# The last batch's stores on GpSimd's queue, and two indirect transfers without an order between them, in an attention and mixture-of-experts kernel

## The chip, the cores and the metric

The kernel runs on one core of one Trainium2 chip. The metric is device microseconds for one execution of the whole program; lower is better. A profile of one execution stands beside the times. Its span runs from the first to the last recorded instruction, and the execution's own time is a little longer than its span.

## The reference

The kernel computes multi-query attention and, on its output, a mixture of experts with a two-step gate. In the reference, cut to what matters:

```python
scores = scale * q @ k.T                       # 8 batches, 16 heads, 384 tokens, head size 64; one k and v per batch
x = softmax(scores) @ v                        # as [3072 tokens, 1024]
g_idx = argmax(x @ w_group)                    # one of 4 groups, weight g_w = its softmax
e_idx = argmax(x @ w_expert[g_idx])            # one of 4 experts in it, weight e_w = its softmax
out[token] = g_w * e_w * (relu(x @ w1[g, e]) @ w2[g, e])
```

Inputs and outputs are float32. Every token goes to exactly one of 16 experts.

## The kernel before, in words

**Attention.** Work goes through 24 tiles of 128 tokens (8 batches, `ST` = 3 tiles each). A written-out loop (L792) runs scores, softmax, transposition and the product with `v` for half a head group at a time; gate steps and loads are hung into its slots with `at`.

**Experts.** For each batch the kernel counts which expert most of a sample of its tokens choose, and runs all 384 tokens of the batch through this one expert; tokens of another expert get the gate value 0 and so rows of zeros. `main_expert` (L535) is a generator: 8 groups of matmuls for the hidden layer (L483, evicted at L489), then for each token tile `j` two halves of 512 columns, each 8 matmuls (L497), evicted into a tile `y` of [128, 1024] float32 by ScalarE (L515) or VectorE (L517). It yields three times for each such group, and `advance(n)` takes `3 * n` steps, so `advance(1)` is one group of 8 matmuls on TensorE. When a tile is complete, `store` (L538) writes it in four transfers of 32 rows, one for each `n`, because token rows lie interleaved: `out_v = out.rearrange("(b j r n) d -> b j n r d", n=4, r=32)`. SP issues them; for the very last tile ScalarE's queue issues two of the four.

**The last batch** has a second expert as well. Up to 32 tokens that chose it are gathered (`few_gather`, L649), run through its weights with the 32 tokens as the stationary side (`few_rows`, L672, called twice in `few_expert`, L683), and their rows are written by an indirect transfer (L694) that takes one row number per partition: 32 tokens by four quarters of a row. It stands after the main expert's stores and overwrites the zero rows that these wrote. `few_places` (L620) computes on VectorE where each of these tokens goes and whether they fit (`fits32`); `few_parts` (L641) and the gate values run on GpSimd.

**Remaining pairs.** A loop at the end (L909) runs once for each pair of batch and expert that is still left; it reloads that batch's hidden input from `xb_scratch`, which `keep_xb` (L473) wrote. On these inputs no instruction of its body is recorded.

**Queues.** Weights are loaded by GpSimd's queue (L458; they are converted from float32 to bfloat16 on the way), which is DMA queue q0. SP's transfers are q1, those of ScalarE's queue q10. Instructions on an engine's queue run in order. The framework orders two transfers that may write the same bytes: the later waits on its issuing engine until the earlier has landed. `manual_schedule` keeps the program order as written.

**The end, in program order** (L888 to L906): `few_gather`, `advance(2)` (tile 0), the list of the remaining pairs, `advance(1000)` (tiles 1 and 2), `keep_xb`, `few_expert`, then the loop.

Of the kernel before, what the change touches and what calls it, by code (L numbers as in the profile page):

```python
# [11 lines left out]
I32 = mybir.dt.int32  # L12
P = 128
AX = mybir.AxisListType
ALU = mybir.AluOpType
ACTF = mybir.ActivationFunctionType
# [3 lines left out]
def kernel(  # L20
# [11 lines left out]
    nc = tc.nc  # L32
# [440 lines left out]
    def keep_xb(b):  # L473
        nc.sync.dma_start(out=xb_dram[b], in_=st["xb", b][:].rearrange("p c t -> p (c t)"))

    def expert(xb, w1, w2, result, psum, on_act=None):

        on_act = on_act or (lambda k: k % 2 == 0)
        h_t = pool.tile([P, FO, S], BF16, tag="hT", bufs=1)
        for fc in range(FO):  # L480
            hp = psum()
            for ko in range(KO):
                nc.tensor.matmul(  # L483
                    out=hp[:, 0:S], lhsT=w1[:, ko, ts(fc, P)], rhs=xb[:, ko, :], start=(ko == 0), stop=(ko == KO - 1)
                )
                if ko % (KO // 2) == KO // 2 - 1:
                    yield
            if on_act(fc):
                nc.scalar.activation(out=h_t[:, fc, :], in_=hp[:, 0:S], func=ACTF.Relu)  # L489
            else:  # L490
                nc.vector.tensor_scalar(out=h_t[:, fc, :], in0=hp[:, 0:S], scalar1=0.0, scalar2=None, op0=ALU.max)
            yield
        for j in range(ST):
            for nh in range(2):
                yp = psum()
                for fo in range(FO):
                    nc.tensor.matmul(  # L497
                        out=yp, lhsT=h_t[:, fo, ts(j, P)], rhs=w2[:, fo, ts(nh, 512)],
                        start=(fo == 0), stop=(fo == FO - 1),
                    )  # L500
                    if fo % (FO // 2) == FO // 2 - 1:
                        yield
                result(j, nh, yp, on_act(FO + 2 * j + nh))
                yield

    def scaled(gcol, store):

        ys = {}

        def result(j, nh, yp, by_act):  # L510
            if nh == 0:
                ys[j] = pool.tile([P, Dm], FP32, tag="y", name="y", bufs=3)
            y, g = ys[j], gcol()[:, j:j + 1]
            if by_act:
                nc.scalar.activation(out=y[:, ts(nh, 512)], in_=yp, func=ACTF.Copy, scale=g)  # L515
            else:
                nc.vector.tensor_scalar(out=y[:, ts(nh, 512)], in0=yp, scalar1=g, scalar2=None, op0=ALU.mult)  # L517
            if nh == 1:
                store(j, y)

        return result
# [13 lines left out]
    def main_expert(b, on_act):  # L535
        w1, w2 = st.pop(("w", b))

        def store(j, y):  # L538
            for n in range(QN):
                queue = nc.scalar if b == B - 1 and j == ST - 1 and n % 2 else nc.sync  # L540
                queue.dma_start(out=out_v[b, j, n], in_=y[32 * n:32 * (n + 1), :])

        yield from expert(st["xb", b], w1, w2, scaled(lambda: st["gsel", b][0], store), any_bank, on_act)

    def few_ready():

        c16 = ppool.tile([P, 4 * S], BF16, tag="pr", name="c16")
        c32 = ppool.tile([P, 2 * S], FP32, tag="pr", name="c32")
        st["few"] = fw = {}
        for name, t, widths in (  # L550
            ("16", c16, (("eye", P), ("tri", P), ("sel", ST * P), ("f", 4), ("cum", 4), ("parts", 5 * ST))),
            ("32", c32, (
                ("cols", P), ("tri", P), ("prod", ST * GE), ("ohs", GE), ("rows", ST), ("rest", ST), ("row", 1), ("pos", 4),
                ("f", ST), ("fits", 1), ("fits4", 1), ("gate", 1), ("low", 1), ("at", 1), ("base", 1),
            )),
        ):
            at_ = 0
            for part, w in widths:
                fw[part + name] = t[:, at_:at_ + w]
                at_ += w  # L560
        nc.gpsimd.iota(
            fw["cols32"], pattern=[[0, FQ], [1, FEW]], base=0, channel_multiplier=0,
            allow_small_or_imprecise_dtypes=True,
        )
        nc.gpsimd.memset(fw["tri32"], 1.0)
        nc.gpsimd.affine_select(
            out=fw["tri32"], in_=fw["tri32"], pattern=[[1, P]], compare_op=ALU.is_gt, fill=0.0, base=0,
            channel_multiplier=-1,
        )
        nc.gpsimd.tensor_copy(out=fw["tri16"], in_=fw["tri32"])  # L570
        nc.gpsimd.tensor_copy(out=fw["eye16"], in_=ident[:])
        nc.gpsimd.memset(c16[:, 2 * P + ST * P:2 * P + ST * P + 8], 0.0)

        rows, parts = fw["rows32"], fw["parts16"].rearrange("p (j t) -> p j t", t=5)
        nc.gpsimd.iota(
            rows, pattern=[[P, ST]], base=(B - 1) * S - NR, channel_multiplier=QN, allow_small_or_imprecise_dtypes=True
        )
        for n in range(QN):
            nc.gpsimd.memset(fw["low32"][32 * n:32 * (n + 1), :], float(n * (1 - 32 * QN)))
        for c in range(FQ):  # L580
            nc.gpsimd.memset(fw["base32"][ts(c, FEW), :], float(FQ * NR + c))
        nc.gpsimd.tensor_tensor(
            out=rows, in0=rows, in1=fw["low32"].to_broadcast([P, ST]), op=ALU.add
        )
        nc.gpsimd.tensor_copy(out=parts[:, :, 3], in_=rows)
        nc.gpsimd.tensor_tensor(out=parts[:, :, 4], in0=rows, in1=parts[:, :, 3], op=ALU.subtract)
        fw["xt"] = [ppool.tile([P, Dm], BF16, tag="pr", name="xtok") for _ in range(ST)]
        xg = ppool.tile([P, 2 * KO * FEW], BF16, tag="pr", name="xg")
        fw["xg"], fw["h16"] = xg[:, 0:KO * FEW], xg[:, KO * FEW:]
        rest = pool.tile([P, 512], FP32, tag="qt", name="rest", bufs=3)  # L590
        fw["h32"], fw["y32"] = rest[:, 0:KO * FEW], rest[:, KO * FEW:]
# [28 lines left out]
    def few_places():  # L620
        fw, ohs = st["few"], st["ohs", B - 1]
        bank = xbank()
        nc.tensor.matmul(out=bank[:, 0:4], lhsT=fw["tri16"], rhs=fw["f16"], start=True, stop=False)
        nc.tensor.matmul(out=bank[:, 0:4], lhsT=ones[:], rhs=fw["cum16"], start=False, stop=True)
        pos = fw["pos32"]
        nc.vector.tensor_copy(out=pos, in_=bank[:, 0:4])
        nc.vector.tensor_single_scalar(out=fw["fits32"], in_=pos[:, 3:4], scalar=float(FEW), op=ALU.is_le)
        nc.vector.tensor_scalar(
            out=fw["fits432"], in0=fw["fits32"], scalar1=float(FQ), scalar2=None, op0=ALU.mult
        )  # L630
        nc.vector.tensor_scalar(
            out=fw["ohs32"], in0=ohs[1], scalar1=fw["fits32"], scalar2=None, op0=ALU.mult
        )
        ohs[1] = fw["ohs32"]
        for j in range(ST):
            nc.vector.tensor_scalar(
                out=fw["sel16"][:, ts(j, P)], in0=fw["cols32"], scalar1=pos[:, j:j + 1], scalar2=fw["f32"][:, j:j + 1],
                op0=ALU.is_equal, op1=ALU.mult,
            )
# [40 lines left out]
                )  # L680
        return bank[:, 0:256]

    def few_expert():  # L683

        fw = st["few"]
        w1, w2 = st.pop("w_second")
        bank = few_rows(fw["xg"], w1)
        nc.vector.transpose(
            out=fw["h32"].rearrange("p (o t) -> p o t", t=FEW), in_=bank.rearrange("p (x o) -> p o x", o=FO)
        )  # L690
        nc.vector.tensor_scalar(out=fw["h16"], in0=fw["h32"], scalar1=0.0, scalar2=None, op0=ALU.max)
        bank = few_rows(fw["h16"], w2)
        nc.vector.tensor_scalar(out=fw["y32"], in0=bank, scalar1=fw["gate32"], scalar2=None, op0=ALU.mult)
        nc.gpsimd.indirect_dma_start(  # L694
            out=out_q, out_offset=bass.IndirectOffsetOnAxis(ap=fw["at32"].bitcast(I32), axis=0), in_=fw["y32"],
            in_offset=None, bounds_check=FQ * N - 1, oob_is_err=False,
        )
# [203 lines left out]
    nc.vector.tensor_copy(out=lsi[:, NP:NP + 1], in_=nsum[:])  # L901
    assert not later

    advance(1000)
    keep_xb(b)
    few_expert()  # L906

    n_rem = nc.values_load(lsi[0:1, NP:NP + 1], min_val=0, max_val=NP)
    with tc.For_i(0, n_rem, 1) as it:  # L909
        free.clear()  # L910
        e = nc.gpsimd.value_load(lse[0:1, ds(it, 1)], min_val=0, max_val=GE - 1)
        w1, w2 = load_w(e, 0), load_w(e, 1)
        bi = nc.sync.value_load(lsb[0:1, ds(it, 1)], min_val=0, max_val=B - 1)
        xr = pool.tile([P, KO, S], BF16, tag="xb", name="xr", bufs=2)
        nc.sync.dma_start(
# [44 lines left out]
```

## Time and profile before

| | us |
|---|---|
| three runs | 505.77, 508.03, 508.03 |
| median | 508.03 |
| the profiled execution | 507.47 |
| its span | 506.0 |

| engine | busy us | share of the span |
|---|---|---|
| TensorE, matmul | 479.9 | 95% |
| VectorE | 412.6 | 82% |
| ScalarE | 319.6 | 63% |
| GpSimd | 288.4 | 57% |

In the profile, PE is TensorE's matmuls and PEld its weight loads, DVE is VectorE, ACT ScalarE, POOL GpSimd, SP SyncE; a `q` behind the name is the engine's instruction queue (waits, DMA issues). A timeline line has the start, the length, the engine, the source line and the operation, the tile written and those read, shapes and a count; in brackets stands how long the engine sat idle before it, and what ended that. "DMA to landing" is the time from a transfer's start on the issuing engine to its completion signal. Tables of DMA queues give packets, MB and the time of the packets as a share of 16 DMA engines over the window.

### The profile page before, as it was taken

The numbers are of one execution on the slowest core, as the hardware profiler recorded it, in microseconds if no ns is written. First come the engines' busy times: TensorE is split into PE (matmuls) and PEld (weight loads), VectorE is DVE, ScalarE is ACT, GpSimd is POOL, SyncE is SP. The second block draws the span as 40 slices with busy tenths as digits, with TensorE's granted clock in tenths as the row PEclk, the third lists the DMA queues.
The fourth block names the chain that finished last, engine by engine and source line by source line (L and its number), as shares of the span: only waits on it lengthen the run. The fifth ranks groups of instructions, "written<-read, shape, count | busy, mean of one in ns | idle before, by whom it ended". The sixth has DMA issues, their size and how long they took to land.

```text
span 506.0 us, 20018 instructions
## 1 busy us (share of the span) xinstructions
PE 479.9 (95%) x8249; PEld 257.5 (51%) x8249; DVE 412.6 (82%) x738; ACT 319.6 (63%) x997; POOL 288.4 (57%) x528
## 2 busy tenths in 40 slices
PE   7687789999999999999999999999999999999992
PEld 3144355555455455555555455554555455555651
DVE  3899979998799888998799888898799888891441
ACT  4776756766765775766765875766766766662420
POOL 1656865585476654685476654684566653674210
PEclk9799999999999999999999999999999999999997
DMA  7522899389955999479965999279964995069995
GB/s 111 121 45 43 150 237 222 74 135 230 252 121 102 208 244 240 80 136 229 242 137 93 203 247 254 54 138 225 227 175 78 197 240 159 3 117 228 242 225 181
DMA packets 63660, 84.04 MB, mean 166 GB/s; under 512 B 20280, under 2 KB 39868, under 8 KB 63312
## 3 DMA queue, kind: packets, MB, share of 16 engines
q0 software_dynamic: 18288, 37.84, 41.2%
q1 hardware_dynamic: 44224, 44.35, 35.1%
q8 instruction: 66, 1.08, 0.9%
q10 hardware_dynamic: 1056, 0.56, 0.5%
q14 instruction: 26, 0.21, 0.1%
HBM read 101.52 MB, written 19.01 MB: 238 GB/s over the span
## 4 chain that ended last, share of the span: by engine, by line
PE 88%; DVE 4%; ACT 2%; DMA 2%; issue 1%; POOL 0%; SPq 0%; POOLq 0%; ACTq 0%; DVEq 0%
PE x L261 26%; PE s L210 26%; PE x L483 15%; PE x L497 13%; PE sb L497 3%; PE x L284 3%; ACT pr L224 2%; DVE nmx L221 2%; PE sb L483 2%; DMA out_dram<-y 2%; DVE ring L245 1%; PE x L104 1%; PE x L149 0%; PE x L187 0%; PE x L598 0%
## 5 line engine op out<-in xcount | busy, mean ns | idle before, releaser
L239 POOL TENSOR_SCALAR pr<-pr,rinv 128x384 f32<-128x384 f32 x384 | 217.3, 585 | 149.1 <-DVE rinv L235 135.9
L224 ACT ACTIVATE pr<-s,nmx 128x384 f32<-128x384 f32 x384 | 218.0, 579 | 132.2 <-DVE nmx L221 122.4
L221 DVE TENSOR_REDUCE nmx<-s 128x2 f32<-128x768 f32 x192 | 174.5, 949 | 47.2 <-PE s L210 46.3
L245 DVE STREAM_TRANSPOSE ring<-pr 128x768 f32<-128x768 f32 x192 | 175.4, 952 | 0.1
L210 PE MATMUL s<-kt,qt 64*64 64x384 f32 x1536 | 151.3, 504 | 12.0 <-ACT pr L224 9.9
L261 PE MATMUL x<-ring,v_sb 32*64 32x256 f32 x4608 | 137.9, 378 | 0.4 <-issue 0.3
L261 PEld LDWEIGHTS x<-ring,v_sb 32*64 32x64 f32 x4608 | 101.2, 131 | 43.7 <-issue 23.7
L210 PEld LDWEIGHTS s<-kt,qt 64*64 64x64 f32 x1536 | 48.8, 133 | 83.0 <-ACT pr L224 44.4
L224 ACT ACTIVATION_READ_ACCUMULATOR pr<-s,nmx 128x1 f32 x384 | 77.8, 203 | 0.0
L483 PE MATMUL x<-xb,w 128*128 128x384 bf16 x448 | 76.6, 326 | 0.0
L483 PEld LDWEIGHTS <-w 128*128 128x128 bf16 x512 | 47.7, 98 | 42.2 <-issue 12.6
L497 PE MATMUL x<-w,h_t 128*128 128x512 bf16 x288 | 65.3, 380 | 0.0
L497 PEld LDWEIGHTS <-h_t 128*128 128x128 bf16 x384 | 35.7, 98 | 51.9 <-issue 11.9
L458 POOL DMA_DIRECT2D w<-in_moe_w_dram x36 | 27.4, 767 | 10.7 <-issue 8.8
L275 ACT COPY xt<-x 128x256 f32<-128x256 f32 x96 | 28.9, 385 | 3.3 <-PE x L261 3.3
L489 ACT ACTIVATE h_t<-x 128x384 bf16<-128x384 f32 x56 | 25.4, 502 | 6.6 <-PE x L483 6.6
L276 POOL CAST xb<-xt 128x1024 bf16<-128x1024 f32 x24 | 24.9, 1036 | 3.4 <-ACT xt L275 3.4
L515 ACT ACTIVATE y<-x,gsel 128x512 f32<-128x512 f32 x36 | 24.8, 693 | 3.1 <-PE x L497 3.1
L199 DVE STREAM_TRANSPOSE qt<-q_sb 128x512 f32<-128x512 f32 x38 | 26.1, 687 | 0.0
L497 PE MATMUL sb<-w,h_t 128*128 128x512 bf16 x96 | 21.5, 379 | 0.0
L235 DVE RECIPROCAL rinv<-ssum 128x4 f32<-128x4 f32 x96 | 13.9, 145 | 3.3 <-ACT pr L224 3.3
L515 ACT ACTIVATE y<-sb,gsel 128x512 f32<-128x512 f32 x9 | 6.2, 689 | 15.7 <-PE sb L497 15.7
(129 smaller groups left out, 153.0 us busy)
## 6 DMA issues: line engine op xcount, KB each, us to landing
w<-in_moe_w_dram POOLq DMA_DIRECT2D x36, 1024.0 KB, 19.4
q_sb<-in_q_dram SPq DMA_DIRECT2D x76, 224.0 KB, 6.0
out_dram<-y SPq DMA_DIRECT2D x94, 128.0 KB, 6.4
xb_scratch<-xb SPq DMA_DIRECT2D x8, 768.0 KB, 4.3
v_sb<-in_v_dram SPq DMA_DIRECT2D x32, 96.0 KB, 3.7
kk<-in_k_dram SPq DMA_DIRECT2D x28, 92.0 KB, 4.1
q_sb<-in_q_dram SPq DMA_DIRECT2D x16, 128.0 KB, 3.4
q_sb<-in_q_dram SPq DMA_DIRECT2D x5, 64.0 KB, 3.0
```

Source lines behind the costliest of these rows:

```text
L199: nc.vector.transpose(out=qt[:].rearrange("p (x d) -> p x d", d=32), in_=q_sb[:, :, 0:32])
L210: nc.tensor.matmul(out=s[m * D:(m + 1) * D, h, 0:S], lhsT=qt[r, ts(2 * cc + m, D)], rhs=kt[r, :], start=True, stop=True, tile_position=(h ...
L221: nc.vector.tensor_reduce(out=nmx[:], in_=s[:, :, 0:S], axis=AX.X, op=ALU.max, negate=True)
L224: nc.scalar.activation(out=pr[:, h, :], in_=s[:, h, 0:S], func=ACTF.Exp, bias=nmx[:, h:h + 1], scale=1.0, accum_out=ssum[:, k, h:h + 1],)
L239: nc.gpsimd.tensor_scalar(out=pr, in0=pr, scalar1=rinv[:, k, h:h + 1], scalar2=1.0, op0=ALU.mult, op1=ALU.mult)
L245: nc.vector.transpose(out=ring[:, (u // 4) % 3, u % 4].rearrange("p h s -> p (h s)"), in_=st.pop(("pr", u))[:].rearrange("p h s -> p (h s)"),)
L261: nc.tensor.matmul(out=o[i][h * D:(h + 1) * D, 0:2 * P].rearrange("d (g c q) -> d g c q", g=2, c=4), lhsT=v_sb[r, n, :], rhs=ring[r, a:z + ...
L275: nc.scalar.copy(out=xt[:, :, ts(i, 32)], in_=o[:, 0:2 * P].rearrange("p (c q) -> p c q", c=KO))
L458: nc.gpsimd.dma_start(out=w[:, o:o + 4, :], in_=views[n][ds(e, 1), :, o:o + 4, :].rearrange("o p c f -> (o p) c f"))
L483: nc.tensor.matmul(out=hp[:, 0:S], lhsT=w1[:, ko, ts(fc, P)], rhs=xb[:, ko, :], start=(ko == 0), stop=(ko == KO - 1))
L497: nc.tensor.matmul(out=yp, lhsT=h_t[:, fo, ts(j, P)], rhs=w2[:, fo, ts(nh, 512)], start=(fo == 0), stop=(fo == FO - 1),)
L515: nc.scalar.activation(out=y[:, ts(nh, 512)], in_=yp, func=ACTF.Copy, scale=g)
```

## The change

- Tile 2 of the last batch is evicted in three pieces of 512, 256 and 256 columns. Its rows are written by an indirect transfer of all 128 rows on GpSimd's queue, with a list `main32` of row numbers in which the second expert's tokens (if they fit) have a number out of bounds, so that their rows are not written. Two VectorE operations in `few_places` make the list.
- `few_expert` is cut in `few_first` and `few_last`. `few_first` now runs after tile 1, `few_last` after the first 512 columns of tile 2. The few rows' indirect transfer is so issued ahead of tile 2's, and the framework is told that the two write no row in common (`declare_no_dep`).
- Tiles 0 and 1 of the last batch are written by one transfer each, on GpSimd's queue.
- `keep_xb` of the last batch moves into the loop.

```diff
         for j in range(ST):
-            for nh in range(2):
-                yp = psum()
+            widths = (512, 256, 256) if split and j == ST - 1 else (512, 512)
+            at_ = 0
+            for n, w in enumerate(widths):
+                yp = psum()[:, 0:w]
...
         def store(j, y):
-            for n in range(QN):
-                queue = nc.scalar if b == B - 1 and j == ST - 1 and n % 2 else nc.sync
-                queue.dma_start(out=out_v[b, j, n], in_=y[32 * n:32 * (n + 1), :])
+            if b < B - 1:
+                for n in range(QN):
+                    nc.sync.dma_start(out=out_v[b, j, n], in_=y[32 * n:32 * (n + 1), :])
+            elif j < ST - 1:
+                nc.gpsimd.dma_start(out=out_v[b, j], in_=y[:])
+            else:
+                main = nc.gpsimd.indirect_dma_start(
+                    out=out, out_offset=bass.IndirectOffsetOnAxis(ap=st["few"]["main32"].bitcast(I32), axis=0),
+                    in_=y[:], in_offset=None, bounds_check=N - 1, oob_is_err=False,
+                )
+                tc.declare_no_dep(
+                    main.ins, st["few_rows"].ins, reason="no row of out is written by both: main32 leaves out the few's"
+                )
...
+        nc.vector.tensor_scalar(
+            out=fw["drop32"], in0=fw["f32"][:, ST - 1:ST], scalar1=fw["fits32"], scalar2=float(NR), op0=ALU.mult,
+            op1=ALU.mult,
+        )
+        nc.vector.tensor_scalar(
+            out=fw["main32"].bitcast(I32), in0=fw["rows32"][:, ST - 1:ST], scalar1=fw["drop32"],
+            scalar2=float(NR), op0=ALU.add, op1=ALU.add,
+        )
...
+    advance(2)
+    few_first()
+    advance(1)
+    few_last()
     advance(1000)
-    keep_xb(b)
-    few_expert()
...
         w1, w2 = load_w(e, 0), load_w(e, 1)
+        keep_xb(B - 1)
```

More of the change, by code (lines that the diff above doesn't have):

```diff
@@ L474, in keep_xb, with expert @@
         nc.sync.dma_start(out=xb_dram[b], in_=st["xb", b][:].rearrange("p c t -> p (c t)"))
-    def expert(xb, w1, w2, result, psum, on_act=None):
+    def expert(xb, w1, w2, result, psum, on_act=None, split=False):
         on_act = on_act or (lambda k: k % 2 == 0)
@@ L493, in expert @@
         for j in range(ST):
-            for nh in range(2):
-                yp = psum()
+            widths = (512, 256, 256) if split and j == ST - 1 else (512, 512)
+            at_ = 0
+            for n, w in enumerate(widths):
+                yp = psum()[:, 0:w]
                 for fo in range(FO):
                     nc.tensor.matmul(
-                        out=yp, lhsT=h_t[:, fo, ts(j, P)], rhs=w2[:, fo, ts(nh, 512)],
+                        out=yp, lhsT=h_t[:, fo, ts(j, P)], rhs=w2[:, fo, at_:at_ + w],
                         start=(fo == 0), stop=(fo == FO - 1),
@@ L502, in expert @@
                         yield
-                result(j, nh, yp, on_act(FO + 2 * j + nh))
+                result(j, at_, w, yp, on_act(FO + 2 * j + n))
+                at_ += w
                 yield
@@ L508, in scaled, with result @@
         ys = {}
-        def result(j, nh, yp, by_act):
-            if nh == 0:
+        def result(j, at_, w, yp, by_act):
+            if at_ == 0:
                 ys[j] = pool.tile([P, Dm], FP32, tag="y", name="y", bufs=3)
@@ L514, in result @@
             if by_act:
-                nc.scalar.activation(out=y[:, ts(nh, 512)], in_=yp, func=ACTF.Copy, scale=g)
+                nc.scalar.activation(out=y[:, at_:at_ + w], in_=yp, func=ACTF.Copy, scale=g)
             else:
-                nc.vector.tensor_scalar(out=y[:, ts(nh, 512)], in0=yp, scalar1=g, scalar2=None, op0=ALU.mult)
-            if nh == 1:
+                nc.vector.tensor_scalar(out=y[:, at_:at_ + w], in0=yp, scalar1=g, scalar2=None, op0=ALU.mult)
+            if at_ + w == Dm:
                 store(j, y)
@@ L538, in store @@
         def store(j, y):
-            for n in range(QN):
-                queue = nc.scalar if b == B - 1 and j == ST - 1 and n % 2 else nc.sync
-                queue.dma_start(out=out_v[b, j, n], in_=y[32 * n:32 * (n + 1), :])
-        yield from expert(st["xb", b], w1, w2, scaled(lambda: st["gsel", b][0], store), any_bank, on_act)
+            if b < B - 1:
[11 more added lines that the diff above has]
+                )
+        result = scaled(lambda: st["gsel", b][0], store)
+        yield from expert(st["xb", b], w1, w2, result, any_bank, on_act, split=(b == B - 1))
     def few_ready():
@@ L554, in few_ready @@
                 ("f", ST), ("fits", 1), ("fits4", 1), ("gate", 1), ("low", 1), ("at", 1), ("base", 1),
+                ("drop", 1), ("main", 1),
             )),
@@ L681, in few_rows, with few_first @@
         return bank[:, 0:256]
-    def few_expert():
+    def few_first():
         fw = st["few"]
-        w1, w2 = st.pop("w_second")
-        bank = few_rows(fw["xg"], w1)
+        bank = few_rows(fw["xg"], st["w_second"][0])
         nc.vector.transpose(
@@ L691, in few_expert, with few_last @@
         nc.vector.tensor_scalar(out=fw["h16"], in0=fw["h32"], scalar1=0.0, scalar2=None, op0=ALU.max)
-        bank = few_rows(fw["h16"], w2)
+    def few_last():
+        fw = st["few"]
+        bank = few_rows(fw["h16"], st.pop("w_second")[1])
         nc.vector.tensor_scalar(out=fw["y32"], in0=bank, scalar1=fw["gate32"], scalar2=None, op0=ALU.mult)
-        nc.gpsimd.indirect_dma_start(
+        st["few_rows"] = nc.gpsimd.indirect_dma_start(
             out=out_q, out_offset=bass.IndirectOffsetOnAxis(ap=fw["at32"].bitcast(I32), axis=0), in_=fw["y32"],
```

## Prediction

> **What bounds the kernel now.** I read the page's head first, then the chain of waits of the last 65 us, then the timeline and the DMA tables of the tail. The change touches nothing ahead of 477 us, so only the tail can pay.
>
> ```profile
> span 506.0 us, 20018 instructions
> ```
>
> The profiled execution took 507.47 us, 1.47 more than its span. The three runs gave 505.77, 508.03 and 508.03; the sum below is made against 507.47 and sits 0.56 under their median.
>
> Chain of waits, window 440 to 507 (start, length, what):
>
> ```profile
> 488.53 6.91 DMA out_dram<-y
> ...
> 496.28 2.91 DMA out_dram<-y
> ...
> 499.21 0.04 POOLq L694
> ...
> 499.51 0.62 issue
> 500.14 0.29 POOLq L908
> 500.43 1.04 POOL out_dram L694
> ```
>
> Until 487 the chain is TensorE; from there it is transfers. The last store of `y` lands at 496.28+2.91=499.19, and only then GpSimd's queue lets L694 go, the indirect transfer of the second expert's rows. L694 in the timeline, then in the view of its line:
>
> ```profile
> 500.36 1.11 POOL L694 DMA_INDIRECT out_dram<-rest,c  x1 [16.84 <-issue]
> ```
>
> ```profile
> DMA to landing us min/median/max: 2.5/2.5/2.5
> ```
>
> So release (499.21) to start is 1.15, the work on GpSimd 1.11, and landing 2.5 after the start, at 502.86. From there to the end of the span are 3.14 us of closing waits. That tail, 499.2 to 506.0, hangs on one event: **every earlier store of `out` has landed**. Call it R; now R=499.2.
>
> What feeds it, from the timeline of all engines:
>
> ```profile
> 483.65 3.61 PE L497 MATMUL sb<-w,h_t 128*128 128x512 bf16 x16
> ...
> 487.15 7.07 PE L497 MATMUL sb<-w,h_t 128*128 128x512 bf16 x32
> 487.36 0.75 DVE L517 TENSOR_SCALAR y<-sb,gsel 128x512 f32<-128x512 f32 x1 [2.70 <-PE x L892]
> ...
> 490.81 0.75 DVE L517 TENSOR_SCALAR y<-sb,gsel 128x512 f32<-128x512 f32 x1 [1.72 <-PE sb L497]
> 492.58 0.69 ACT L515 ACTIVATE y<-sb,gsel 128x512 f32<-128x512 f32 x1 [2.77 <-PE sb L497]
> 494.15 1.06 PE L677 MATMUL x<-w,xg 128*32 128x256 bf16 x32
> 494.26 0.75 DVE L517 TENSOR_SCALAR y<-sb,gsel 128x512 f32<-128x512 f32 x1 [2.70 <-PE sb L497]
> ...
> 496.09 1.06 PE L677 MATMUL x<-w,xg 128*32 128x256 bf16 x32 [0.88 <-DVE xg L691]
> ```
>
> TensorE turns out the last batch's three token tiles (16 matmuls each) from 483.65 to 494.2, then L677 twice for the few rows. Tile 0 of `y` is complete at 488.11, tile 1 at 491.56, tile 2 at 495.01. The DMA engines are still busy with the second expert's `w2`. Its two loads in the view of L458, window 470 to 500; then the DMA queues in 488 to 490, in 490 to 495.26 and in 502 to 506 (packets, MB, share of 16 engines):
>
> ```profile
> L458 POOL DMA_DIRECT2D w<-in_moe_w_dram x2: 547/570/593, 470.3 to 470.9; - x2
> ...
> DMA to landing us min/median/max: 19.4/21.9/24.4
> ```
>
> ```profile
> q0 software_dynamic: 60, 0.43, 104.0%
> ```
>
> ```profile
> q0 software_dynamic: 90, 0.61, 55.4%
> q1 hardware_dynamic: 256, 0.71, 34.3%
> ```
>
> ```profile
> q0 software_dynamic: 48, 0.09, 6.1%
> ...
> q1 hardware_dynamic: 1, 0.00, 0.0%
> ```
>
> Issued 0.6 apart, the loads land at 489.7 and 495.3, 5.6 apart: q0, GpSimd's queue, takes them one after the other, and in 488 to 490 it alone fills the engines (104%). Beside the second, q1 (SP's queue) carries stores of `y` for 34.3% of 5.26 = 1.8 us of each engine. The last q0 row is L694's own data; none of it moves before 502.0, 0.55 after GpSimd ended at 501.47, and it takes 6.1% of 4 = 0.24 us.
>
> **The change, part by part.**
>
> *Two small VectorE operations in few_places.* From the timeline:
>
> ```profile
> 477.98 0.15 DVE L627 TENSOR_SCALAR c<-c 128x1 f32<-128x1 f32 x1
> 478.17 0.15 DVE L628 TENSOR_SCALAR c<-c 128x1 f32<-128x1 f32 x1
> ...
> 479.71 0.21 POOL L425 TENSOR_TENSOR gw<-wt 128x12 f32<-128x12 f32 x1 [6.74 <-DVE wt L422]
> ...
> 483.32 0.20 POOL L647 TENSOR_TENSOR c<-c,c 128x3 bf16<-128x3 f32 x1
> ...
> 483.57 0.22 PE L662 MATMUL x<-c 128*128 128x5 bf16 x3
> ```
>
> One such operation costs 0.19 from start to start, two 0.4. GpSimd waits for VectorE at L425, works on to L647 (ends 483.52), and L662 on TensorE starts 0.05 later, so nothing hides them there: between 0 and 0.4, I take 0.4, and every tile of `y` is that much later. Behind it stands a larger cover: the stores can't start before `w2` is through (below). Worth 0 at the end; 0.4 if `w2` were early.
>
> *Tiles 0 and 1: one transfer each on GpSimd's queue in place of four each on SP's.* Removed: eight issues on SP, which no one waits for afterwards. Added: two issues on GpSimd, 0.57 each by the L458 row, on an engine that idles 16.84 us there. What matters is the queue. On q1 the stores slipped in between the packets of `w2`; on q0 they stand behind them. Without q1's 1.8, `w2` lands between 493.5 and 495.3 (nothing given back); I take 493.7. From 490 on, q0 had 55.4% of 5.26 = 2.9 us of work per engine, so the average engine is through at 492.9. Tile 1 is ready at 492.0 with the 0.4; 0.1 to start, 0.57, and 0.55 to the first packet give 493.2. I start both stores at 493.5.
>
> How long they take is the disputed price. By q1's row 0.71 MB cost 34.3% of 5.26 us on 16 engines = 28.9 engine-us, 40.7 per MB. A tile of 0.524 MB is 21.3 engine-us: **1.33 us on all sixteen engines, 5.3 us on four.** Both ends come from that row. In the old store (L541) both sides count 32 rows outermost, in the weights' loads (L458) both count 128. The new store has 128 partitions on the SBUF side, but on the DRAM side n=4 outermost, then r=32: a common cut of both along their outermost index has only four shares. No transfer of the trace has sides so different, so no row vouches for sixteen; the nearest one, L541, has the same four-fold n, taken apart by hand into four transfers. I take four engines, and for the second store the next four (the other way is a rival). They then run side by side: 493.5 + 5.3, and 0.5 from the last packet to the landing (L694: 502.86 − 502.0 − 0.24 is 0.6 at most), so **R = 499.3** (497.8 to 500.7 with `w2` and packet times at their ends).
>
> [...]
>
> *few_first and few_last moved into tile 2.* TensorE's 64 matmuls of L677 (2 × 1.06) now run before tile 2's end; the VectorE steps between them (0.88 of TensorE's waiting in the last row above) lie beside the 8 matmuls of tile 2's first half (7.07/4 = 1.77). Tile 1's matmuls end at 490.8+0.4=491.2; L677 to 492.3; half a tile to 494.0; the second L677 needs all of `w2`, 493.7, no wait (1.3 if it landed at 495.3); to 495.1; the two halves of 256, 1.77 (twice that if a matmul of half the width cost as much; but L677 does 32 of width 256 in 1.06), 496.9; the eviction of 128×256 costs between 0 and the 0.69 of 128×512 on ScalarE, I take 0.4. Tile 2 is ready at 497.3 (up to 500.7 with all of these against it) where it was 495.0, and the few rows near 495.6 where it was 497.7. Neither is last: both wait on GpSimd's queue for R.
>
> *Two indirect transfers.* few_last's transfer may overwrite rows of tiles 0 and 1, so it still waits for R; the main one stands behind it on GpSimd's queue and needs no landing of it. After R: 1.15, then 1.11 for the few, 1.11 for tile 2 (also 128 indices), 0.55 to the first packet, 1.33 for 0.524 MB on all engines, 0.5 to land: 5.75. Before it was 502.86 − 499.2 = 3.66. So 2.1 are added: a second generation and a larger transfer, which before lay ahead of R.
>
> *keep_xb into the loop.* 768 KB leave the tail: SP issued them behind the last `y` on the same queue,
>
> ```profile
> 497.13 0.35 SPq L474 DMA_DIRECT2D xb_scratch<-xb  x1
> ```
>
> and when the few's data moved, from 502.0 on, q1 had one packet left. So they neither held R up nor the few; worth 0. The loop itself doesn't run on these inputs.
>
> **Sum.** 499.3 + 5.75 = 505.05 landing, + 3.14 = 508.2 of span, + 1.47 = **509.7 us**, 2.2 over the profiled 507.47 (R +0.1, the second indirect transfer +2.1). The wait for the order is gone, but the wait for the stores stays, and what follows it is longer.
>
> **The rivals.**
>
> *Sixteen engines.* The two stores go one after the other over all engines: 493.7 + 2 × 1.33 + 0.5 = R 496.9, everything else as above: 505.8 of span, **507.3 us**, no change. For it: L694's and the weights' data spread evenly. Against it: the unlike sides. The gain in R (2.3) is what the second transfer costs (2.1).
>
> *The same four engines twice*, the slower side. If both stores get the same share of engines, tile 1 queues behind tile 0 there: R = 493.5 + 10.6 + 0.5 = 504.6, and 513.5 + 1.47 = **515.0 us**. It decides from the moment that tile 1's first packet waits for tile 0's last; nothing in the trace excludes it.
>
> *The order is kept after all.* If the main transfer waits for the landing of the few, then R + 3.66 + 1.15 + 1.11 + 0.55 + 1.33 + 0.5 = R + 8.3, **512.2 us**. Against it: the declaration in the code names just this pair.
>
> **How the numbers follow.** Forecast 0.58, sixteen engines 0.22, same four twice 0.12, order kept 0.05, something else 0.03. The forecast's own range is 508.2 to 511.1. The range 505.8 to 513.0 takes in the sixteen and the kept order, and leaves out the same four twice and the outer tails, about 0.18. A measurement of this kernel can tell some 0.5% (2.5 us) from no change. Slower by more: the same four, the kept order, and about a third of the forecast, 0.37. Faster by more would need R under 494.6, or a cheaper end: 0.07. The rest, 0.56, lies within.
>
> **What would show it.** Right: the stores of `y` on GpSimd's queue land over 5 us after `w2` does, the DMA share in 494 to 499 is near half, not full; GpSimd shows two indirect transfers in succession 1.15 after R; the last landing is 5.7 after R. Sixteen engines would show both stores landed by 497 and a full DMA share. Wrong would be: R under 496.5, a gap over 1.5 between the two indirect transfers, a generation for tile 2 far from 1.11, or TensorE waiting over 1.5 for `w2`.

## The result and the profile after

| | before | after |
|---|---|---|
| median of 5 runs, us | 506.94 | 511.51 |
| lowest to highest | 505.54 to 508.03 | 510.88 to 512.56 |
| ratio | | 1.0092, 95% interval 1.0064 to 1.012 |
| profiled execution, us | 507.47 | 512.56 |
| its span | 506.0 | 511.1 |

The changed kernel is slower, 4.6 us by the medians and 5.1 by the spans. What stands ahead of the tail differs from run to run (in the traces of this document tile 0's eviction ends between 485.9 and 488.7), so the tails are compared from one mark in each trace: the end of tile 0's eviction (before 487.36 + 0.75 = 488.11; after in the row below, 487.76). "R" is, as in the prediction, the landing of the last direct store of the last batch.

| us after tile 0's eviction | before | after |
|---|---|---|
| second expert's `w2` landed | 7.2 | 6.4 |
| tile 2 evicted | 6.9 | 9.4 |
| R | 11.1 | 14.4 |
| few rows' transfer starts on GpSimd | 12.3 | 15.3 |
| last landing | 14.7 | 20.1 |
| end of the span | 17.9 | 23.4 |

Of 5.5 us, 3.3 come ahead of R, 2.1 lie between R and the last landing, 0.1 in the closing waits. In the changed kernel, GpSimd's timeline from 484 on and, ahead of it, the eviction that is the mark (start, length, engine, line, operation; in brackets the idle time before and its releaser):

```profile
487.01 0.75 DVE L520 TENSOR_SCALAR y<-sb,gsel 128x512 f32<-128x512 f32 x1 [2.70 <-PE x L920]
```

```profile
488.39 0.79 POOL L546 DMA_DIRECT2D out_dram<-y  x1 [5.21 <-DVE lsi L922]
491.81 0.69 POOL L546 DMA_DIRECT2D out_dram<-y  x1 [2.63 <-issue]
503.10 1.11 POOL L722 DMA_INDIRECT out_dram<-rest,c  x1 [10.60 <-DMA out_dram<-y]
504.52 1.00 POOL L548 DMA_INDIRECT out_dram<-y,c  x1 [0.31 <-issue]
```

L546 are the one-transfer stores of tiles 0 and 1, L722 the few rows, L548 tile 2. Before, GpSimd's idle time ahead of L694 was charged to "issue"; now 10.60 us of it are charged by name to a store of `y`. The view of L546 has how long those stores took from issue to landing, and the DMA tables of 494 to 498 and of 498.4 to 502 what moved (packets, MB, share of 16 engines):

```profile
DMA to landing us min/median/max: 10.0/10.1/10.3
```

```profile
q0 software_dynamic: 341, 0.60, 49.0%
```

```profile
q0 software_dynamic: 58, 0.22, 16.1%
```

Tile 0's store lands at 498.3, tile 1's at 502.15. Between 494 and 498 hardly anything but these two is under way, and the engines are at 49%: as much as eight of sixteen. After tile 0 has landed, tile 1 goes on alone, and in its last 3.6 us the share is 16%, less than four engines: from 500.0 to 501.8 it is 10%, so not all of its engines end at the same time. Before, the engines were at 98 to 100% from 496 to 500, with the stores of `y` and with `xb_scratch`. So the wait didn't go; it is now a wait for two stores that leave at first half of the DMA engines idle, later more.

TensorE's wait for the second product's weights, and ScalarE's last piece of tile 2:

```profile
494.22 0.62 PE L702 MATMUL x<-w,xg 128*32 128x256 bf16 x16 [0.42 <-DMA w<-in_moe_w_dram]
```

```profile
496.73 0.47 ACT L518 ACTIVATE y<-sb,gsel 128x256 f32<-128x256 f32 x1 [2.71 <-PE sb L499]
```

`w2` holds TensorE up for 0.42 us, and tile 2 is ready at 497.2, seven microseconds ahead of the transfer that writes it (504.52).

### The profile page after: what moved, and what is told of

Read it like the earlier page. It is cut to its first block, busy times and chain, and to the rows that moved or that the text cites. A ratio compares the mean times of both kernels' runs of the same rounds, so it can differ in the third digit from the quotient of the medians.

```text
span 511.1 us, 20028 instructions
## 1 busy us (share of the span) xinstructions
PE 478.4 (94%) x8257; PEld 258.0 (50%) x8257; DVE 413.0 (81%) x740; ACT 319.7 (63%) x998; POOL 292.2 (57%) x531
## 2 busy tenths in 40 slices
DMA packets 64140, 83.23 MB, mean 163 GB/s; under 512 B 20894, under 2 KB 40482, under 8 KB 63792
## 5 line engine op out<-in xcount | busy, mean ns | idle before, releaser
L458 POOL DMA_DIRECT2D w<-in_moe_w_dram x36 | 27.5, 773 | 10.8 <-issue 9.0
L499 PE MATMUL sb<-w,h_t 128*128 128x512 bf16 (+1 forms) x104 | 21.8, 363 | 0.0
L518 ACT ACTIVATE y<-sb,gsel 128x512 f32<-128x512 f32 (+1 forms) x10 | 6.7, 667 | 19.9 <-PE sb L499 19.9
## 6 DMA issues: line engine op xcount, KB each, us to landing
out_dram<-y POOLq DMA_DIRECT2D x2, 512.0 KB, 10.1
```

Source lines behind the costliest of these rows:

```text
L458: nc.gpsimd.dma_start(out=w[:, o:o + 4, :], in_=views[n][ds(e, 1), :, o:o + 4, :].rearrange("o p c f -> (o p) c f"))
L499: nc.tensor.matmul(out=yp, lhsT=h_t[:, fo, ts(j, P)], rhs=w2[:, fo, at_:at_ + w], start=(fo == 0), stop=(fo == FO - 1),)
L518: nc.scalar.activation(out=y[:, at_:at_ + w], in_=yp, func=ACTF.Copy, scale=g)
```

## The experiments

Each ratio below is to the kernel before, run again beside that version; its median was then between 505.6 and 505.9. Times after tile 0's eviction are from one trace of each version.

Theory A at the start: a transfer that counts 4 on its outermost DRAM dimension runs on four engines, and this sets R. Its rival B: standing behind `w2` on GpSimd's queue is what costs.

### Four transfers per tile, on GpSimd's queue

```diff
             elif j < ST - 1:
-                nc.gpsimd.dma_start(out=out_v[b, j], in_=y[:])
+                for n in range(QN):
+                    nc.gpsimd.dma_start(out=out_v[b, j, n], in_=y[32 * n:32 * (n + 1), :])
```

> The changed kernel, with tiles 0 and 1 of the last batch stored by four transfers of 32 rows each, still on GpSimd's queue. Theory A (one transfer with 4 as its outermost count runs on four DMA engines, and this sets R): the stores land near 497.3 instead of 502.2, the last landing follows 5.7 later, so 4.9 us come off the changed kernel: about 506.7 us, ratio to the kernel before 0.995 to 1.003. Theory B (standing behind w2 on GpSimd's queue is what costs): nothing comes off, 511.5 us, ratio 1.009.

Measured: 507.58 us, ratio 1.0021 (1.0001 to 1.0041). The stores of both tiles (L547, the last one issued at 494.53), GpSimd's last two rows, and the DMA table of 494 to 496:

```profile
DMA to landing us min/median/max: 2.2/4.3/5.6
```

```profile
497.88 1.13 POOL L723 DMA_INDIRECT out_dram<-rest,c  x1 [2.86 <-issue]
499.31 0.99 POOL L549 DMA_INDIRECT out_dram<-y,c  x1 [0.30 <-issue]
```

```profile
q0 software_dynamic: 213, 0.58, 89.3%
```

The same bytes on the same queue, in pieces whose outermost count is 32 on both sides, fill the engines (89%) and have landed at 494.53 + 2.2 = 496.7, 8.4 after tile 0's eviction: R is 6 us earlier than in the changed kernel, and the intervals of the two ratios lie apart. B falls. The end of the span comes 5.1 earlier (the landing 0.2 and the closing waits 0.7 us slower than in the changed kernel's profile).

### Four transfers per tile, on SP's queue

```diff
-                nc.gpsimd.dma_start(out=out_v[b, j], in_=y[:])
+                for n in range(QN):
+                    nc.sync.dma_start(out=out_v[b, j, n], in_=y[32 * n:32 * (n + 1), :])
```

> The changed kernel, with tiles 0 and 1 of the last batch stored by four transfers each on SP's queue, as in the kernel before. Theory A: as with four transfers on GpSimd's queue within 1 us, about 506.7 us; the stores share the engines with w2, which lands near 495.3, TensorE waits about 1 us for it, and the stores land near 497.2. Theory B (the queue costs): 506.7 us here and 511.5 us with four transfers on GpSimd's queue.

Measured: 505.76 us, ratio 0.9997 (0.9977 to 1.0017). R came 9.0 after tile 0's eviction, `w2` landed at 7.0, tile 2 was evicted at 10.1 and the end was at 18.0, against 18.3 on GpSimd's queue. Which queue issues the small stores matters little, as A has it. This is the changed kernel without its one-transfer stores, and it's as fast as the kernel before: the reordering alone brings and costs nothing that can be measured.

### The one-transfer stores alone

```diff
         def store(j, y):
+            if b == B - 1 and j < ST - 1:
+                nc.gpsimd.dma_start(out=out_v[b, j], in_=y[:])
+                return
             for n in range(QN):
```

> The kernel before, with only the stores of tiles 0 and 1 of the last batch made one transfer each on GpSimd's queue. Theory A: R moves from 499.2 to about 502.2, and what follows R stays 3.66 to the landing, so 3.0 us more than the kernel before: 509.9 us, ratio 1.006; the rest of the changed kernel's loss (about 2) is the second indirect transfer. Rival (the loss comes from the two indirect transfers or from the moved matmuls): 507 us, ratio 1.000.

Measured: 512.52 us, ratio 1.0129 (1.0098 to 1.0161). This one edit to the kernel before costs 6.5 us, as much as the whole change: the two intervals overlap, and in its trace, that of the fastest run of four, the end stands 5.0 us further behind tile 0's eviction than in the kernel before, in the changed kernel's 5.5. The theory had the sign and half the size. Tile 2's stores (L544, issued by SP and ScalarE from 493.2 on):

```profile
DMA to landing us min/median/max: 8.4/8.5/8.6
```

Tile 2's four transfers, of the shape that kept the engines at 89% above, now take 8.5 us where the kernel before had 2.1 to 3.1; they land at 502.2, when the one-transfer stores are through on their engines (the second lands at 501.4). R came 16.0 after tile 0's eviction against 11.1, the end at 22.9 against 17.9. The few rows' transfer starts 1.25 after R.

### The order kept

```diff
-                tc.declare_no_dep(
-                    main.ins, st["few_rows"].ins, reason="no row of out is written by both: main32 leaves out the few's"
-                )
```

> The changed kernel without the declaration that the two indirect transfers write no row in common, so that tile 2's waits until the few rows have landed. By the sum on record this adds 2.5 us to the changed kernel (R + 8.3 against R + 5.75): 514 us, ratio 1.014. Rival (the two follow one another slowly anyway, through GpSimd's queue): 511.5 us, ratio 1.009.

Measured: 513.03 us, ratio 1.0136 (1.0101 to 1.017).

```profile
501.87 1.10 POOL L719 DMA_INDIRECT out_dram<-rest,c  x1 [11.13 <-DMA out_dram<-y]
505.23 1.00 POOL L548 DMA_INDIRECT out_dram<-y,c  x1 [2.25 <-DMA out_dram<-rest,c]
```

GpSimd waits 2.25 between the two in place of 0.31, and the end comes 25.8 after tile 0's eviction in place of 23.4. Of these 2.4 us, 0.5 stand ahead of R (14.9 in place of 14.4), where the edit changes nothing; from R to the last landing there are 7.65 in place of 5.71. The declaration does what it says and is worth 1.9 us by the traces, where the prediction's sum has 2.5; the two intervals of the ratios overlap, so the medians alone would not show it.

### One transfer per tile on SP's queue

```diff
-                nc.gpsimd.dma_start(out=out_v[b, j], in_=y[:])
+                nc.sync.dma_start(out=out_v[b, j], in_=y[:])
```

> The changed kernel with tiles 0 and 1 of the last batch stored by one transfer each on SP's queue. Theory A: the count of four is a matter of the transfer, not of GpSimd's queue, so these are slow as well. If SP's queue gives both stores the same four engines, they stand behind each other and beside w2's packets: landed 15 to 16 us after the end of tile 0's eviction, 512 to 513 us. If it gives them different ones: about 10 to 11, 508 us. Rival (only GpSimd's queue splits by four): landed at 9, as with four transfers on SP, 506 us.

Measured: 512.39 us, ratio 1.0125 (1.0101 to 1.0148). DMA table of 493 to 501:

```profile
DMA packets 212, 0.87 MB, mean 109 GB/s; under 512 B 4, under 2 KB 4, under 8 KB 210
...
q1 hardware_dynamic: 210, 0.84, 25.6%
```

For eight microseconds a quarter of the engines (25.6%) is busy, though two stores are waiting: as if both stood on the same four. 0.84 MB in 8 us on four engines is 5.0 us for a tile, the price in the prediction. The few rows' transfer starts at 503.47, 16.25 after tile 0's eviction. So the count of four is a matter of the transfer's shape, and the prediction's slower rival fits what SP's queue did here: 25.6% is what both stores on the same four engines would give, 49.0% in the changed kernel what two stores on different ones would. Which engines they are no run here shows.

### Tile 1 alone, tile 0 alone

In the changed kernel the second one-transfer store took longer than the price of 5 us: from `w2`'s landing to R there are 8.0. Theory A1: the two stores hinder each other. In each kernel one tile is stored by one transfer and the other by four:

```diff
+            elif j == 0:        # the other kernel: j == 1
+                for n in range(QN):
+                    nc.gpsimd.dma_start(out=out_v[b, j, n], in_=y[32 * n:32 * (n + 1), :])
             elif j < ST - 1:
                 nc.gpsimd.dma_start(out=out_v[b, j], in_=y[:])
```

> The changed kernel with tile 0 stored by four transfers of 32 rows and only tile 1 by one transfer, all on GpSimd's queue. Counted from the end of tile 0's eviction, the stores had landed at 14.4 in the changed kernel and at 8.5 with both tiles in four transfers. Theory A1 (the two one-transfer stores hinder each other while both run): tile 1 alone takes its 5.3 us on four engines after w2 and tile 0's 1.3, landed at about 12.3; time about 2 us under the changed kernel, 509.5. Theory A2 (tile 1's transfer is slow by its place in the queue or its time): landed at 14.4 or later, 511.5 us.

> The changed kernel with only tile 0 stored by one transfer and tile 1 by four transfers of 32 rows, all on GpSimd's queue. Theory A1: tile 0 takes 5.3 us on four engines from about 5 us after its eviction (landed at 10.8), and tile 1's shares on these four engines stand behind it: landed at about 12, time about 509 us. Theory A2: as without any delay of tile 1, landed at 10.8, 508 us.

Measured: tile 1 alone in one transfer 511.1 us, ratio 1.0092 (1.0067 to 1.0117); tile 0 alone 509.36 us, ratio 1.0061 (1.0039 to 1.0084). Tile 1's store (L549, issued at 492.18):

```profile
DMA to landing us min/median/max: 10.2/10.2/10.2
```

Without tile 0's one transfer beside it, tile 1's still needs 10.2 us and R is at 14.3, as in the changed kernel. A1 falls. Tile 0's alone lands 4.3 us after `w2`, and R (tile 1's small stores, which land from 10.3 on) is at 11.2, between the 10.8 and the 12 of the two theories: the small stores did end behind the four long shares, but by little.

### Which engines read what

Most 4-KB packets of these stores take 0.159 us. In the trace of tile 1 alone, 17 of those after 495.1 took 0.3 to 0.7 us, nearly all in twos that began within 0.1 us of each other. Theory A3 made of it (with 0.33 us for such a packet) that two engines reading partitions 32 apart hinder each other. Tile 0 goes in four transfers and tile 1 in three, one of which has 64 partitions:

```diff
-                nc.gpsimd.dma_start(out=out_v[b, j], in_=y[:])
+                for n, m in ((2, 1), (3, 1), (0, 2)) if j else ((0, 1), (1, 1), (2, 1), (3, 1)):
+                    dst = out_v[b, j, n] if m == 1 else out_v[b, j, n:n + m]
+                    nc.gpsimd.dma_start(out=dst, in_=y[32 * n:32 * (n + m), :])
```

The second kernel has `((0, 1), (3, 1), (1, 2))`.

> The changed kernel with tile 0 in four transfers of 32 rows, and tile 1 in three: n=2 and n=3 with 32 rows each, and n=0,1 together (64 partitions, outermost count 2), all on GpSimd's queue. Theory A3 (tile 1's transfer is slow where two of its engines read partitions 32 apart at the same time, in step: pages of packets of 330 ns starting together in pairs, against 159 ns for one): the pair runs at 330 ns a packet until something sets its engines apart, 32 packets take between 7 and 10.6 us, landed at 14 or later after tile 0's eviction. Theory A4 (whatever slows tile 1 has to do with its time or its place in the queue): as the next kernel, within 0.5 us.

> As the kernel before it in this list, but with n=0 and n=3 apart and n=1,2 together (partitions 32 to 95, also two engines by the count of two). Theory A3: these two engines read partitions 32 to 63 and 64 to 95; if it is halves of 64 partitions within which two engines hinder each other, these two do not: 159 ns a packet, 32 packets in 5.1 us, landed near 12. Theory A4: as with n=0,1 together.

One run each: 511.13 and 511.62 us. Issue to landing of the seven stores, n=0,1 together and then n=1,2 together:

```profile
DMA to landing us min/median/max: 3.4/5.3/9.1
```

```profile
DMA to landing us min/median/max: 3.8/5.7/8.4
```

The pair is the slowest in both, 9.1 and 8.4, and R is at 14.2 and 13.5, where A3 had 12 for the second. The partitions make little difference, and A3 falls in the form in which it was put. An outermost count of 2 on 64 partitions costs nearly as much as 4 on 128 (R 14.3): each engine has 32 packets either way (in the first run the share is 13% of sixteen from 496 to 498, two engines).

### Tile 1's one transfer in quiet

Left were A5, that the other engines' work on tile 2 slows it, and A6, that it is slow by itself. Here tile 0 goes in four transfers, tile 1's store is issued at tile 2's and waits for the landing of tile 2's rows, and `few_last` comes last; the store runs when the compute engines have nothing left.

```diff
+            elif j == 1:
+                st["y1"] = y
...
+                late = nc.gpsimd.dma_start(out=out_v[b, 1], in_=st.pop("y1")[:])
...
     few_first()
-    advance(1)
-    few_last()
     advance(1000)
+    few_last()
```

> The changed kernel with tile 0 in four transfers, few_last behind tile 2, and tile 1's one-transfer store issued last but for the few rows, after tile 2's rows have landed, when TensorE, ScalarE and VectorE have nothing left to do. It is made to time this transfer in quiet; the kernel is slower for it. Theory A5 (tile 1's one transfer is slowed while the other engines finish tile 2): in quiet its 128 packets take 5.3 us on four engines, and issue to landing is 6.5 to 7.0 us. Theory A6 (it is slow at its start whenever it starts, for reasons of its own): 128 packets take 7 us or more, issue to landing 8.5 us or more.

One run, 519.86 us. The view of the store (L557, issued at 501.38), and the DMA tables of 502.7 to 503.5, of 503.5 to 508 and of 508 to 511.5:

```profile
DMA to landing us min/median/max: 10.4/10.4/10.4
```

```profile
DMA packets 407, 0.05 MB, mean 58 GB/s; under 512 B 396, under 2 KB 396, under 8 KB 407
```

```profile
q0 software_dynamic: 59, 0.24, 24.5%
```

```profile
q0 software_dynamic: 62, 0.24, 16.7%
```

10.4 us with nothing beside it: A5 falls, A6 holds. The data move from 502.7 to 511.4, 8.7 us for one tile, where SP's queue needed 5.0 for the same tile on four engines. In the middle window four engines are busy (24.5% of sixteen) but move only 59 packets of 4 KB in 4.5 us: 24.5% × 4.5 × 16 / 59 is 0.30 us a packet, on SP's queue 25.6% × 8 × 16 / 210 is 0.16. From 508 on a packet takes the usual time again (58 of 4 KB beside 4 small ones, 0.16), but from 509.5 to 511.5 the share is 12%, two engines. So the loss has two parts: long packets in the first 5.3 us, and engines that don't end together. And there are 396 packets under 512 bytes, that is 12 × 33; SP's stores had 4 in their 8 us. They are all through by 503.5, 4.5 us before the packets of 4 KB are back at their usual length, so they don't slow them by running beside them. In the changed kernel's page the count of such packets rose from 20280 to 20894, though it has ten transfers fewer.

### Lists for all three tiles

The lists leave the second expert's tokens out of all three tiles, so that no transfer of the last batch waits for another's landing.

```diff
-            elif j < ST - 1:
-                nc.gpsimd.dma_start(out=out_v[b, j], in_=y[:])
             else:
                 main = nc.gpsimd.indirect_dma_start(
-                    ... ap=st["few"]["main32"].bitcast(I32), axis=0),
+                    ... ap=st["few"]["main32"][:, j:j + 1].bitcast(I32), axis=0),
                     in_=y[:], in_offset=None, bounds_check=N - 1, oob_is_err=False,
                 )
+                apart(main)   # declare_no_dep with every earlier one of these transfers
```

> All three tiles of the last batch written by indirect transfers whose lists leave out the second expert's tokens, each declared free of rows in common with the others and with the few rows' transfer; the lists are made after few_gather, off TensorE's path. Nothing then waits for a landing. Theory: the last landing hangs on tile 2's eviction (9 us after tile 0's): 0.8 to start, 1.0 of GpSimd, 2.35 to land, 3.25 of closing waits, end at 16.4 from tile 0's eviction against 17.9 in the kernel before: 1.5 us faster than the kernel before, ratio 0.996 to 0.998. Rival (an indirect transfer of a whole tile is split on few engines too, or is held up by the ones ahead on GpSimd): end at 18 or later, ratio 1.000 or more.

Measured: 505.49 us, ratio 0.9988 (0.9972 to 1.0005). GpSimd's last two rows:

```profile
495.49 0.98 POOL L727 DMA_INDIRECT out_dram<-rest,c  x1 [2.84 <-DVE rest L725]
497.33 0.96 POOL L546 DMA_INDIRECT out_dram<-y,c  x1 [0.85 <-ACTq L946]
```

The few rows go as soon as they are there, tile 2 starts 0.3 after its eviction, and whole-tile indirect transfers are not slow. The end is at 17.25 against 17.9: 0.6 in place of 1.5, since tile 2 was evicted at 9.7, not 9.0, and its rows took 4.0 to land, not 3.3. It is not shown to be faster than the kernel before.

### The same, with the few rows' second product behind tile 2

```diff
     few_first()
-    advance(1)
-    few_last()
     advance(1000)
+    few_last()
```

> The kernel with lists for all three tiles, with few_last moved behind tile 2's last matmul, so that tile 2 does not stand behind the second expert's second product and does not wait for w2. Theory: tile 2 is ready at about 8.0 after tile 0's eviction instead of 9.4, its rows land at 12.3, the few rows at about the same time, the end is at 15.6 against 17.9 in the kernel before: 2.2 us faster than it, ratio 0.994 to 0.998. Rival (the few rows' transfer, now issued last, sets the end): end at 16.9 or later, as with the lists alone, ratio 0.998 to 1.000.

Measured: 506.34 us, ratio 1.0000 (0.9984 to 1.0016). The view of L546, and the DMA table of 496 to 500.5:

```profile
DMA to landing us min/median/max: 4.9/5.1/7.2
```

```profile
q8 instruction: 1, 0.02, 1.7%
```

Tile 2 was indeed evicted at 7.9, but its rows took 4.9 to land and the closing waits 4.4 in place of 3.25, so the end came at 17.6. The theory fails. The rival's end (16.9 or later) and ratio fit, its reason only in part: the few rows did land last, but only 0.2 behind tile 2. What made the closing waits longer is open. One packet of instruction loading stood on one engine for 1.7% of 4.5 us times 16, 1.2 us, just when tile 2's rows began; that this is why they landed late is an inference from one trace. No version was faster than the kernel before beyond its interval.

## Why the prediction was right in its direction and range, and short in its size

- **The forecast's mechanism held.** The stores ran side by side with as much as eight engines busy (49.0%; one store alone, 24.5%), so four each, and different ones; that they would be different ones was the author's choice, with no row of the kernel before for it. Both stores in four pieces take 6 us off R. The sixteen-engine rival is out; the rival with the same four twice fits what the same edit does on SP's queue (25.6%); the kept order isn't what happened; put back, it cost 1.9 behind R, 2.5 by its sum. One sign of being right failed for one store: tile 0's landed 4.2 after `w2`, not over 5.
- **The step that failed is "5.3 us on four" for tile 1.** The prediction priced both stores by q1's packets. Tile 0's was about right: it landed 4.2 us after `w2` (expected 5.6). Tile 1's landed 8.0 after it, and R came 14.4 after tile 0's eviction where the sum has 499.3 − 488.5 = 10.8. That is 3.6 too little: 1.2 is `w2`, which landed at 6.4 in place of 5.2, and 2.4 the store. The time was off by less, 511.51 by the median against 509.7, and 511.1 of span against 508.2, because tile 0's eviction ended 0.7 earlier than the sum had it; that part is luck. The price was read from SP's queue, where it holds (5.0 per tile), and carried to GpSimd's, where the same transfer, alone and in quiet, moved data for 8.7 us (10.4 from issue to landing).
- **What follows R held.** R to the last landing was 5.71 (expected 5.75), and the closing waits 3.25 (3.14). Its terms were 0.95 from R to the start for 1.15, 0.31 between the two transfers for nothing, 1.00 of work for tile 2 for 1.11 and 2.34 to its landing for 2.38; that these errors cancel to 0.04 is luck.
- **The small steps.** VectorE's two operations cost 0.4 on their engine, and L662's successor on TensorE waited 0.27 for GpSimd, near the 0.4 taken. TensorE waited 0.42 for `w2` where 0 was taken, within the bound of 1.3. The eviction of 256 columns took 0.47 (0.4), tile 2 was ready 9.4 after tile 0's eviction (497.3 − 488.5 = 8.8 in the sum; that the clock times, 497.2 and 497.3, agree comes of the earlier eviction). All of it was hidden by R, as stated.
- **What stays open** is why such a store is slow on GpSimd's queue. Interference between the two stores, the work of the other engines and the pairing of partitions were each tried and fell. Tile 0's store, which had stood behind `w2` for some four microseconds, was not slow; that a store which reaches free engines soon after its issue is slow at its start fits all traces, but no run settled the cause. The 12 × 33 small packets don't run beside the slow ones for long (they are through 0.8 us after the data begin); whether what issues them slows the rest is not shown, since they weren't taken away alone.

## What to carry to other kernels

When transfers are merged, look at the outermost count that both sides are left with: four transfers of 32 rows kept the engines at 89%, one transfer over the same bytes with an outermost 4 used a quarter of them (24.5% and 25.6%), and two such put R 6 us later, where the rest of the change brought nothing that could be measured (ratio 0.9997). A wait that is taken away pays only as far as the next one in line: here both indirect transfers hung on the landing of the direct stores, and with the stores in four pieces each, landed by 9.0 after tile 0's eviction in place of 14.4, the whole reordering came out even. Price a transfer from a row of the queue that will carry it: the same store moved its data in 5.0 us on SP's queue and in 8.7 on GpSimd's.

## What the runs showed of the hardware that wasn't expected

- A store of 512 KB on four engines moved its data in 5.0 us on SP's queue (0.16 us a packet of 4 KB) and in 8.7 on GpSimd's, with nothing beside it (0.30 us a packet up to 5.3 us after the first, then 0.16).
- On GpSimd's queue a four-engine store came with 396 packets under 512 bytes, all within 0.8 us of its start (396 is 12 × 33; on which engines they ran no trace shows); two such stores on SP's queue had 4 in 8 us.
- Behind two four-engine stores on GpSimd's queue, tile 2's four stores on SP's and ScalarE's took 8.5 us in place of 2.1 to 3.1, and landed at 502.2, 0.8 after the second of the two.
- Two indirect transfers in succession, 128 indices each, start 1.3 to 1.4 us apart on GpSimd (1.0 to 1.1 of work and 0.3 between them): 1.42 where the first has rows of 1 KB, 1.27 where it has rows of 4 KB.
